# Sigmoid attention followed by a SiLU layer: halves of queries in the first two batches, loads cast by the DMA, q at both row halves, and another order of the second product

## Chip, cores and metric

The kernel runs on one core of one Trainium2 chip. The metric is the device time of one execution in microseconds (us). Times are medians; traces are of one profiled execution, whose span is some 2 us shorter than its time.

## The reference

Eight batches of 12 heads, 448 positions, head width 64; then a layer with 768 inputs, 2048 hidden units, 768 outputs, over 3584 tokens.

```python
scores = scale * np.matmul(q, k.transpose(0, 1, 3, 2)) - np.log(S)
attn = 1.0 / (1.0 + np.exp(-scores))
attn_out = np.matmul(attn, v)                       # (8, 12, 448, 64), inputs float32
x = attn_out.transpose(0, 2, 1, 3).reshape(B * S, H * D)
h = x @ w_in                                        # 3584 x 768 x 2048
out = (h * (1.0 / (1.0 + np.exp(-h)))) @ w_out      # 3584 x 2048 x 768
```

## The kernel before

The kernel works in float16 with float32 sums. Four heads make a group n, three groups a batch, 24 groups in all. For each group TensorE makes seven steps of scores S (four 64 x 64 products side by side in the array), ScalarE the sigmoids of each step (128 x 896), TensorE V (28 matmuls), VectorE moves the result out as xt. G1 is the product of a batch with w_in: 96 matmuls of 448 columns. G2 is the product with w_out for two blocks of 128 tokens; it is done by Strassen's scheme in Winograd's form, with 7 products of 8 matmuls (384 columns), so it needs sums of its inputs (`gs`, VectorE) and combinations of its products (`ua`, `ub`, `uc`, VectorE). There are 14 such pairs. wi and wo are the copies of w_in and w_out that TensorE reads; xk and xq are the loaded k and q, kT and qT their transposes, and k3 means k of group 3.

Where k and q come from: SP loads float32 into a stage, VectorE or GpSimd casts, then the chunks are transposed, by TensorE for groups 0 to 2 and by the DMA afterwards.

```python
def load_qk(b, g):                       # SP queue, float32 stage
    ... nc.sync.dma_start(t, src[b, 4 * g : 4 * g + 4].rearrange(...))
def cast(b, g, eng_name, eng): ...       # 128 x 896, float32 to float16
def transpose_dma(b, g):                 # one per group for q, one for k
    ... nc.sync.dma_start_transpose(tT[nm][n % NT_], x16[nm][n % 1]...)
```

The order of G2's products and of the stages:

```python
prod(1, X, a11, b11, True, ...);  copy X -> ra
prod(6, Y, s2, t2, True, ...);    comb(rb, Y, ra, "u2")
prod(5, Z, s1, t1, True, ...)
prod(2, X, a12, b21, False, ...); copy X -> o1
prod(7, Y, s3, t3, False, [u2]);  comb(rc, Y, ra, "u3"); comb(o2, Z, rc, "c22")
prod(4, Y, a22, t4, False, [u3]); comb(o2, Y, ra, "c21")    # waits for u3 at once
prod(3, Z, s4, b22, False, [c22]); comb(o1, Z, rb, "c12")
...
plan = [("1", 0), ("1", 1), ("2", 0), ("2", 1), ("2", 2), ("1", 2), ("2", 3), ("2", 4), ("1", 3), ("2", 5), ...]
```

TensorE works in order: an instruction that waits holds all behind it. So the order in which the program lists S, V, G1 and G2 decides what a wait costs.

## Time and profile before

| | before |
|---|---|
| time | 436.48 us (436.12 to 436.83) |
| TensorE busy | 385.4 us of 434.4 |
| ScalarE, VectorE busy | 224.1 and 195.0 us |
| batch 0's attention alone | 0 to 40 us |
| end of G1 of batch 1 | 109.6 us |
| last matmul ends | 429.1 us |

How to read the profile: the page cuts the span into 40 slices and gives each engine's busy share in tenths; sums by stage give the busy time between two moments; the waits list says for whom an engine waited (total, times, longest); the timeline lists instructions with the idle time before them in brackets. In the DMA view q0, `software_dynamic`, is GpSimd's queue, and q1, `hardware_dynamic`, is SP's, which has the DMA transposes. The lines themselves stand in the prediction.

### The profile page before, as it was taken

The numbers are of one execution on the slowest core, as the hardware profiler recorded it, in microseconds if no ns is written. First come the engines' busy times: TensorE is split into PE (matmuls) and PEld (weight loads), VectorE is DVE, ScalarE is ACT, GpSimd is POOL, SyncE is SP. The second block draws the span as 40 slices with busy tenths as digits, with TensorE's granted clock in tenths as the row PEclk, the third lists the DMA queues.
The fourth block names the chain that finished last, engine by engine and source line by source line (L and its number), as shares of the span: only waits on it lengthen the run. The fifth ranks groups of instructions, "written<-read, shape, count | busy, mean of one in ns | idle before, by whom it ended". The sixth has DMA issues, their size and how long they took to land.

```text
span 434.4 us, 7192 instructions
## 1 busy us (share of the span) xinstructions
PE 385.4 (89%) x2938; PEld 187.2 (43%) x2938; DVE 195.0 (45%) x298; ACT 224.1 (52%) x326; POOL 69.9 (16%) x92
## 2 busy tenths in 40 slices
PE   2768977799997999899999999989999999899894
PEld 1333533244443444444454444544444454455452
DVE  2321861244553444734455534634563445545642
ACT  1655475587652668456645556457755434014300
POOL 6344013322003213300121022200210000000000
PEclk9856985699998999999999999999999999999999
DMA  8999987797257898718881388717820220031022
GB/s 226 271 238 205 190 155 165 168 152 151 42 156 151 223 191 180 149 21 201 158 212 23 77 163 191 146 17 132 216 44 10 65 74 0 9 92 48 0 73 73
DMA packets 68513, 54.93 MB, mean 126 GB/s; under 512 B 41344, under 2 KB 64896, under 8 KB 68480
## 3 DMA queue, kind: packets, MB, share of 16 engines
q1 hardware_dynamic: 56512, 42.68, 40.5%
q0 software_dynamic: 11968, 11.80, 18.9%
q8 instruction: 23, 0.38, 0.4%
q14 instruction: 10, 0.08, 0.0%
HBM read 45.61 MB, written 11.01 MB: 130 GB/s over the span
## 4 chain that ended last, share of the span: by engine, by line
PE 78%; DVE 9%; ACT 5%; DMA 4%; issue 1%; SPq 1%; POOL 0%; DVEq 0%; POOLq 0%
PE gm L516 34%; PE gm L653 27%; PE att L406 9%; PE att L388 7%; ACT at L398 5%; DVE gs L250 3%; DVE xt L418 3%; DMA stq<-in_q_dram 2%; DVE uc L664 2%; DMA stk<-in_k_dram 2%; DMA kT<-xk 1%; PE gm L315 1%; DVE ob L664 1%; ACT sg L496 0%; SPq L204 0%
## 5 line engine op out<-in xcount | busy, mean ns | idle before, releaser
L398 ACT ACTIVATE at<-att 128x896 f16<-128x896 f32 x168 | 145.0, 917 | 92.1 <-PE att L388 92.1
L516 PE MATMUL gm<-xt,wi 128*128 128x448 f16 x768 | 151.8, 355 | 0.0
L502 DVE TENSOR_TENSOR gt<-gm,sg 128x448 f16<-128x448 f32 x128 | 79.7, 624 | 79.2 <-ACT sg L496 78.9
L496 ACT ACTIVATE sg<-gm 128x448 f16<-128x448 f32 x128 | 70.0, 547 | 74.4 <-PE gm L516 67.1
L516 PEld LDWEIGHTS <-wi 128*128 128x128 f16 x768 | 73.4, 98 | 76.4 <-issue 12.0
L388 PE MATMUL att<-qT,kT 64*64 64x448 f16 x672 | 57.8, 394 | 18.5 <-ACT at L398 9.8
L653 PEld LDWEIGHTS <-gt 128*128 128x128 f16 x448 | 41.3, 98 | 47.8 <-issue 24.0
L653 PE MATMUL gm<-wo,gt 128*128 128x384 f16 x336 | 61.2, 327 | 0.0
L418 DVE TENSOR_SCALAR xt<-att 128x896 f16<-128x896 f32 x24 | 26.2, 1092 | 69.8 <-PE att L406 69.7
L292 POOL CAST xq<-stq 128x896 f16<-128x896 f32 x21 | 19.6, 932 | 215.1 <-DMA stq<-in_q_dram 202.3
L653 PE MATMUL gm<-so,gs 128*128 128x384 f16 x224 | 40.6, 327 | 7.7 <-DVE gs L250 7.5
L653 PEld LDWEIGHTS <-gs 128*128 128x128 f16 x336 | 31.0, 98 | 35.9 <-DVE gs L250 12.3
L406 PE MATMUL att<-at,v 64*64 64x448 f16 x672 | 43.5, 403 | 1.6 <-ACT at L398 1.6
L388 PEld LDWEIGHTS <-kT 64*64 64x64 f16 x672 | 16.5, 110 | 51.6 <-issue 43.5
L406 PEld LDWEIGHTS <-v 64*64 64x64 f16 x672 | 21.7, 119 | 20.6 <-issue 10.2
L653 PE MATMUL gm<-so,gt 128*128 128x384 f16 x112 | 22.8, 338 | 8.5 <-DVE uc L664 8.4
L664 DVE SCALAR_TENSOR_TENSOR uc<-gm,ua 128x384 f32<-128x384 f32 x14 | 7.8, 556 | 40.4 <-PE gm L653 40.4
L292 POOL CAST xk<-stk 128x896 f16<-128x896 f32 x21 | 20.1, 956 | 13.3 <-DMA stk<-in_k_dram 6.8
L653 PE MATMUL gm<-wo,gs 128*128 128x384 f16 x112 | 21.4, 333 | 0.0
L214 POOL DMA_DIRECT2D v<-in_v_dram x24 | 17.5, 729 | 2.4 <-DMA wi<-in_moe_w_in_dram 2.3
L683 ACT ACTIVATE ob<-gm 128x384 f32<-128x384 f32 x14 | 6.9, 495 | 17.6 <-PE gm L653 17.6
L675 ACT ACTIVATE ua<-gm 128x384 f32<-128x384 f32 x14 | 6.9, 492 | 16.1 <-PE gm L653 16.1
(29 smaller groups left out, 112.3 us busy)
## 6 DMA issues: line engine op xcount, KB each, us to landing
stq<-in_q_dram SPq DMA_DIRECT2D x24, 448.0 KB, 5.3
stk<-in_k_dram SPq DMA_DIRECT2D x24, 448.0 KB, 6.0
out_dram<-ob SPq DMA_DIRECT2D x56, 192.0 KB, 2.9
v<-in_v_dram POOLq DMA_DIRECT2D x24, 224.0 KB, 4.7
wi<-in_moe_w_in_dram POOLq DMA_DIRECT2D x16, 192.0 KB, 11.7
wo<-in_moe_w_out_dram POOLq DMA_DIRECT2D x4, 768.0 KB, 16.5
qT<-xq SPq DMA_TRANSPOSE x21, 3.0
kT<-xk SPq DMA_TRANSPOSE x21, 5.2
```

What stands on the lines that cost most here:

```text
L214: lambda: nc.gpsimd.dma_start(v16[b % NV][:, 2 * g : 2 * g + 2], v[b, 4 * g : 4 * g + 4].rearrange("(j h) (p c) d -> (h p) j (c d)", h=2, ...
L250: return lambda: eng.tensor_tensor(o, a, b_, op)
L292: lambda xi=xi, t=t, e_=e_: e_.tensor_copy(xi.rearrange("p c j d -> p j c d"), t.rearrange("p j (c d) -> p j c d", c=NCH)),
L388: nc.tensor.matmul(pt[64 * h : 64 * h + 64, j, :S], kT[64 * j : 64 * j + 64, s, 64 * h : 64 * h + 64], qT[64 * j : 64 * j + 64, :, 64 * h ...
L398: lambda: nc.scalar.activation(av[:, :, s, :], pt[:, :, :S], AF.Sigmoid, bias=NEG_LOG_S, scale=QKSCALE),
L406: nc.tensor.matmul(pt[64 * j : 64 * j + 64, h, :S], v16[b % NV][64 * h : 64 * h + 64, 2 * g + j, c * D : (c + 1) * D], av[64 * h : 64 * h ...
L418: lambda: nc.vector.tensor_scalar_mul(x[:, 2 * g : 2 * g + 2, :], pt[:, :, :S], SX),
L496: lambda: nc.scalar.activation(t, src, AF.Sigmoid, scale=ISX),
L502: lambda: nc.vector.tensor_tensor(o, src.rearrange("p (a t) -> p a t", t=cn), t.rearrange("p (a t) -> p a t", t=cn), ALU.mult),
L516: nc.tensor.matmul(bank[:, :S], wi[:, cc, fc * P : (fc + 1) * P], x[:, cc, :], start=(cc == 0), stop=(cc == NCC - 1),)
L653: nc.tensor.matmul(bank[:, :HE], lhs[:, c, :], rhs[:, c, :], start=first and c == 0, stop=(c == HFC - 1), skip_group_check=True,)
L664: lambda: nc.vector.scalar_tensor_tensor(o, bank[:, :HE], ISX, u, ALU.mult, ALU.add), prio=-1,
```

## The change

Five things are changed together:

1. In batches 0 and 1 the queries are done in two parts, 256 and 192, so that G1 of the first part can start while the second part's attention is still going on.
2. q and k are loaded by GpSimd's queue with a cast by the DMA; the stage and 48 casts vanish, and loads run several groups ahead.
3. Without the cast the chunks can't be rearranged, so each chunk of q must lie at both row halves of the array. For that q is transposed twice, the second time shifted by 64 columns: three DMA transposes per group (7 + 7 + 8 chunks) in place of two.
4. In G2 product 7 stands ahead of product 2; the sums for a pair are queued ahead and are made inside the pair before; no pair directly follows the G1 that it reads.
5. Warm-up matmuls on zeros, 7 at the start and 19 where waits are expected.

The core of the diff (condensed: helpers, buffer counts and the planning code are cut):

```diff
-                pl.op("SP", 60, ("st", nm, b, g), ...,
-                    lambda t=t, src=src: nc.sync.dma_start(t, src[b, 4 * g : 4 * g + 4].rearrange(...)))
+    def load_k(n): ... nc.gpsimd.dma_start(xk[n % NX]..., src(k, b, g))
+    def load_q(n, part=None): ... nc.gpsimd.dma_start(xq[n % NX][:, D : D + 2 * S]..., src(q, b, g)[:, :, lo:hi])
...
+    def transpose_dma(n):
+        nc.sync.dma_start_transpose(kT[n % NTR], xk[n % NX])
+        nc.sync.dma_start_transpose(qT[n % NTR][:, 1 : NCK : 2], xq[n % NX][:, D : D + 2 * S])
+        nc.sync.dma_start_transpose(qT[n % NTR][:, 0 : NCK + 1 : 2], xq[n % NX])
...
-        prod(2, X, a12, b21, False, [kk("a")])
         prod(7, Y, s3, t3, False, ...)
+        prod(2, X, a12, b21, False, [kk("a")])
         prod(4, Y, a22, t4, False, [kk("u3")] ...)
...
+    order_in = [('k', 0), ('id',), ('q', 0, 0), ('k', 1), ..., ('wi', 0), ('wi', 1), ('wi', 2),
+                ('n', 3), ('n', 4), ('n', 5), ('wo', 0, 4), ('wo', 8, 12), ...]
+    todo += [('S', 0, 0, 0), ..., ('V', 2, 1), ('S', 3, 0, 0), ..., ('S', 4, 0, 0), ('V', 3, 0), ...]
+    items += [G2(0), G2(1), G1(2), G2(2), G2(3), G1(3), G2(4), G2(5), G1(4), G2(6), ...]
```

`order_in` is the order on the GpSimd queue; ('n', 3) loads k, q, v of group 3 and queues its three transposes on SP. `todo` is the attention of batches 0 and 1 in steps, laid between the blocks of G1.

## The prediction

> **What bounds the kernel now.** I read the page's 40 slices first, then the sums by stage, the chain of waits, the waits of TensorE after 110 us, and the DMA packets. The program is: 24 groups n (8 batches of 3, four heads each) of attention, S (scores) then V; a first product G1 per batch (96 matmuls of 448 columns); then G2, 14 pairs of output blocks at 56 matmuls of 384 columns.
>
> ```profile
> PE   2768977799997999899999999989999999899894
> ACT  1655475587652668456645556457755434014300
> PEclk9856985699998999999999999999999999999999
> DMA  8999987797257898718881388717820220031022
> ```
>
> Slices are 10.9 us. TensorE is full from the eleventh on, at nearly full clock. The loss lies in the first ten slices and in small gaps later. The sums by stage (busy us of TensorE, weight loads, VectorE, ScalarE, GpSimd; then the clock, DMA share, GB/s):
>
> ```profile
> 0.00:40.00 40.00, 22.91 (x211) 11.21 (x212) 9.41 (x14) 19.28 (x23) 19.55 (x33) 0.77 1.10 238
> 40.00:59.00 19.00, 19.00 (x96) 9.45 (x95) 14.83 (x21) 8.16 (x15) 2.07 (x3) 0.95 1.12 170
> 59.00:85.00 26.00, 18.09 (x170) 7.46 (x170) 5.59 (x7) 18.06 (x22) 6.46 (x9) 0.63 0.80 178
> 85.00:110.00 25.00, 25.00 (x184) 10.95 (x183) 12.39 (x19) 18.97 (x30) 6.64 (x8) 0.98 0.82 147
> 110.00:430.00 320.00, 300.40 (x2282) 148.14 (x2280) 152.75 (x239) 159.59 (x238) 35.20 (x41) 0.99 0.47 104
> ```
>
> Up to 40 us there is batch 0's attention alone, then G1 of batch 0 alone, from 59 to 85 us batch 1's attention alone; only from 85 us on do attention and products lie side by side. In both lonely attention stages ScalarE works 18 to 19 us, and TensorE is half used and cold. The chain of waits shows the hand-offs in the first:
>
> ```profile
> 13.83 3.35 ACT at L398 x4
> 17.23 2.28 PE att L406 x28
> 19.60 1.10 DVE xt L418
> 20.75 0.59 PE att L388 x4
> ```
>
> Later TensorE idles 19.6 us of the 320 between 110 and 430, mostly here (total, times, longest):
>
> ```profile
> PE gm L653 <- DVE uc L664: 8.4, 12, 1.0
> PE gm L653 <- DVE gs L250: 7.5, 7, 1.5
> PE att L388 <- DMA kT<-xk: 2.4, 1, 2.4
> ```
>
> So there are about 45 us to win at the start and 18 later. After the last matmul some 4.4 us of store remain in any case.
>
> **What the Trainium skill says.** TensorE: Matmul & The Clock Gate, Part 1, gives half clock until about 3.4 us of sustained work, and again after an idle window. The trace agrees: the clock row falls to 0.5 to 0.6 in the attention stages. The same page, Back-to-back issue gap, gives N/2.4 + 2.5 ns for an isolated stream, 189 ns at 448 columns: 12 matmuls of G1 take 2.38 us in the chain (198 ns each with one change to attention and back), so I take its form for 256 and 192 columns as an estimate, 109 and 83 ns. DMA: Bandwidth & Descriptors, section SWDGE vs HWDGE vs iDMA, says that a cast needs the GpSimd path, a DMA transpose the other, and that each DMA engine goes round-robin between the queues. The trace agrees to the packet. Between 41 and 54 us wo streams on the GpSimd queue while two transposes wait on the other:
>
> ```profile
> q0 software_dynamic: 1425, 2.13, 94.4%
> q1 hardware_dynamic: 1418, 0.35, 23.1%
> ```
>
> One transpose packet goes through per wo packet. A transpose has 896 packets of 256 bytes; alone, 928 packets were done in about 1.4 us (68.0 to 69.4 us), here 109 per us, 8 us a transpose. This decides my number.
>
> **The change, part by part.**
>
> 1. *Halves of queries in batches 0 and 1.* Part 0 has 256 queries, part 1 has 192. The order of instructions puts part 0 of groups 0 to 2 first, then G1 of batch 0 part 0 with part 1's attention between its blocks, then G1 part 1 with groups 3 to 5 part 0, then G1 of batch 1 part 0 with their part 1, then G1 of batch 1 part 1 with group 6. First S: k0 and q0 are now issued behind the identity at about 1.4 us and land near 5 and 6; two sets of transposes and two copies put S at about 8.5, against 10.5 before. Part 0 is 3584 sigmoid elements per partition per group; 1792 elements cost 1.66 us by two of the old 0.83 us instructions, and instructions are fewer, so 3.7 us a group plus 0.4 for V's hand-off: 12.3 us for three, end at 21, G1 starts near 23 (before: 40). G1 part 0: 96 x 109 ns = 10.5 us, S and V of part 1 in it 4.4, some 15 changes at 0.24 us 3.6: 18 us. The weights wi land for good at about 31 (27 us of loads at the 200 to 213 packets per us seen when the GpSimd queue is alone), costing 1 to 2 us: end about 42. Next stage likewise about 18, then 18, then G1 part 1 (8.0) with group 6 and changes, 12.5. If every load were there: 42 + 18 + 18 + 12.5 = 90 us. In the kernel before the end of G1 of batch 1 is at 109.5, with six steps of S more done (1.8 us).
>
> 2. *Warm-up matmuls* (7 at the start and some in later waits) keep the clock up; they stand in idle time and cost nothing by themselves.
>
> 3. *Casts by the DMA.* 48 casts leave GpSimd and VectorE (0.93 us each on GpSimd, off the path except for 0.95 in the chain). q and k now go on the GpSimd queue, 256 packets each, at 0.73 us of issue per DMA; 82 DMAs are 60 us of GpSimd time, hidden. The loads run up to four groups ahead, so the one stall at 130 us (2.4) goes.
>
> 4. *q at both row halves* turns two DMA transposes per group into three (7 + 7 + 8 chunks, 2816 packets); 63 in place of 42. Alone that is 4.2 us per group against about 13 us of TensorE work per group: hidden later. Not at the start. Group 3's transposes can begin when k3 lands, about 33 us. Behind it the GpSimd queue has k4 to v5 and all of wo, about 1600 packets at 125 per us in turns (estimated from the v loads, which got 119 to 129) and 2048 at 109 to 113. Taken strictly in turns group 3 is ready at 33 + 13 + 11 = 57 us (wanted at 42); group 4, with the loads of groups 6 and 7 in its way, near 79; group 5 near 90. From group 5 on 37.5 us of work follow to the end of G1 of batch 1 (5 for its part 0, 20 for the next stage, 12.5): 127 us. That would lose 18 us instead of winning 20.
>
> 5. *G2's order and early sums.* The order is now products 1, 6, 5, 7, 2, 4, 3, so a product lies between each combination and the one that needs it (1.3 us, against 0.57 + 0.04 of VectorE); the sums of the next pair start inside the last, and in the plan no pair directly follows the G1 that it reads. So 8.4 + 7.5 + 2.4 = 18.3 us go. From 109.5 on: 324.9 - 18.3 + 1.8 = 308.4, plus 2 for new small waits: 310.
>
> Sum: 90 + 310 = 400 with free transposes, 127 + 310 = 437 with strict turns. I choose group 5 ready at 68 us, between: GpSimd issues at most eight loads ahead and pauses, in which transposes run at full speed, and a kernel with so finely ordered loads was probably fitted on a chip. Then 68 + 37.5 = 105.5, and 105.5 + 310 = 415.
>
> **The rivals.**
> - *The transposes take the place of the wait removed* (437, strict turns). For it: the two equal packet counts, and 50% more transposes. Against it: in the kernel before, groups 3 and 4 still came through by 63.7 us beside wo.
> - *Loads hidden, ScalarE and TensorE balanced* (about 400). For it: slack of the later DMA, whose share after 110 us is 0.47. Against it: DMA share above 1 for the whole first 59 us.
> - *Small matmuls bound by weight loads.* A weight load is 98 ns in the table, a 192-column matmul 83: 96 x 2 x 15 ns = 3 us more. Against it: with 448 columns loads overlap freely. It would add 3 to any of the above.
> - *G2 waits come back* through the one set of sums or the eight result buffers: up to 8 us.
>
> **Range and chances.** I give 40% to about 400 (395 to 410), 35% to the middle (410 to 426), 25% to strict turns (426 to 440). Faster by 2% means under 427.7. Range 394 to 436; faster 0.73, within 2% 0.23, slower 0.04.
>
> **What would show it right or wrong.** Right: G1 starts near 23 us; TensorE waits for DMA transposes qT or kT at groups 3, 4 and 5, between 40 and 70 us, with equal packet counts of both queues; G1 of batch 1 ends at about 105; waits of G2 for uc and gs fall from 15.9 to under 3 us; TensorE idles under 5 us after that. Wrong, to the good: no transpose wait over 2 us, time about 400. Wrong, to the bad: group 5's scores start past 85 us, or the G2 waits stay.

## More of the kernel before

One trap matters later: a matmul's end is modelled. A matmul of 384 columns is recorded with 326 ns although the next one starts 163 ns after it.

## The result

| | before | after |
|---|---|---|
| time, median of 4 | 436.65 us | 425.56 us (424.53 to 425.98) |
| span of the profiled run | 434.4 us | 423.7 us |
| G1 of batch 0 starts | 39.9 us | 22.5 us |
| end of G1 of batch 1 | 109.6 us | 121.9 us |
| from there to the end | 324.8 us | 301.8 us |

The ratio is 0.9744, with a 95% interval of 0.9724 to 0.9764. A ratio is the mean time of one kernel's runs over that of the other's of the same rounds, so it is not quite the ratio of the medians quoted.

The changed kernel starts G1 17 us earlier, yet it ends G1 of batch 1 12 us later; then it wins 23 us. The page of the changed kernel shows where, with the same four rows as before (a slice is now 10.6 us):

```profile
PE   7998013799999999999999999999999999999995
ACT  2865003477775567546655577667645656034100
PEclk9999658699999999999999999999999999999999
DMA  8999999949999983869746998651322100330143
```

TensorE is nearly full in the first four slices, which is the gain that was meant. In slices 5 and 6 (counted from 0) all engines nearly stand still, while the DMA row stays at 9; slices 7 and 8 have a second, smaller hole. From slice 9 on TensorE is at 9 until the last slice. The sums by stage, in the same columns as before:

```profile
0.00:22.50 22.50, 19.80 (x300) 11.10 (x300) 7.61 (x21) 12.55 (x15) 17.46 (x31) 1.00 1.09 159
22.50:41.00 18.50, 17.51 (x260) 11.32 (x256) 7.02 (x11) 11.26 (x18) 9.07 (x14) 1.00 1.22 196
41.00:61.50 20.50, 0.01 (x1) 0.01 (x1) 2.08 (x3) 0.60 (x1) 2.65 (x4) 0.59 1.18 199
61.50:122.00 60.50, 50.60 (x693) 34.88 (x694) 25.95 (x40) 36.23 (x56) 12.86 (x18) 0.89 1.13 148
122.00:419.00 297.00, 296.79 (x2308) 148.84 (x2306) 149.48 (x237) 162.92 (x243) 22.93 (x32) 1.00 0.54 97
```

Between 41 and 61.5 us TensorE does 0.01 us of work. After 122 us it idles 0.2 us of 297. The longest of what TensorE waited for, by the waits list of the whole span (the four left out are 0.4 us and less):

```profile
PE att L407 <- DMA qT<-xq: 29.9, 2, 20.5
PE gm L841 <- DVE warm L195: 1.2, 1, 1.2
PE gm L346 <- DMA xk<-in_k_dram: 0.7, 1, 0.7
PE gm L579 <- DMA wi<-in_moe_w_in_dram: 0.7, 1, 0.7
```

The waits of G2 for `uc` and `gs` are gone from the list. In their place stand two waits for the transposed q, groups 3 and 4. The timeline of SP's queue gives each DMA transpose's issue (start, duration); three lines are a group, k then q then q shifted:

```profile
33.18 1.33 SPq L325 DMA_TRANSPOSE kT<-xk  x1
34.57 4.57 SPq L329 DMA_TRANSPOSE qT<-xq  x1
39.19 9.37 SPq L333 DMA_TRANSPOSE qT<-xq  x1
48.68 7.66 SPq L325 DMA_TRANSPOSE kT<-xk  x1
...
77.10 1.24 SPq L325 DMA_TRANSPOSE kT<-xk  x1
78.45 1.43 SPq L329 DMA_TRANSPOSE qT<-xq  x1
```

Group 3's first transpose is issued as soon as k3 has landed (33.1 us), and its last has landed at 61.4 us. Over the whole run the median of an issue is 1.25 to 1.31 us; here it takes up to 9.4. I read this as the issue itself standing in line behind packets that move slowly; no run tests that. The DMA view between 41 and 54 us, the same window as the prediction showed of before (queue: packets, MB, share):

```profile
q0 software_dynamic: 1605, 2.19, 94.3%
q1 hardware_dynamic: 1605, 0.39, 24.1%
```

The two counts are equal. Counted over 36 to 60 us the transposes got 2818 packets, about the 2816 of one group, the first at 37.1 us. Between 76 and 78 us, when GpSimd's queue moves only 25 packets, the transposes get 2091 in 2 us.

The kernel before had transposes as slow as this: those of group 3 landed at 50.4 and 57.7 us. But there G1 of batch 0 kept TensorE busy until 59.1 us, so nobody waited. The change asks for the same group at 41 us.

### The profile page after: what moved, and what is told of

It is laid out like the page before. It is cut to its first block, busy times and chain, and to the rows that moved or that the text cites. A ratio compares the mean times of both kernels' runs of the same rounds, so it can differ in the third digit from the quotient of the medians. Undisturbed runs are those within 1.5% of the kernel's fastest.

```text
span 423.7 us, 8550 instructions
## 1 busy us (share of the span) xinstructions
PE 384.7 (91%) x3555; PEld 206.1 (49%) x3555; DVE 192.5 (45%) x311; ACT 223.5 (53%) x332; POOL 65.0 (15%) x97
## 4 chain that ended last, share of the span: by engine, by line
PE 82%; DMA 10%; SPq 4%; POOL 1%; DVE 1%; issue 1%; ACT 1%; POOLq 0%; ACTq 0%
PE gm L579 34%; PE gm L665 31%; PE att L407 9%; PE att L419 8%; DMA wi<-in_moe_w_in_dram 4%; DMA qT<-xq 4%; SPq L325 2%; DMA v<-in_v_dram 2%; SPq L333 1%; SPq L329 1%; POOL xk L215 1%; POOL xq L224 0%; DVE gs L272 0%; ACT at L812 0%; ACT sg L537 0%
## 5 line engine op out<-in xcount | busy, mean ns | idle before, releaser
L579 PE MATMUL gm<-xt,wi 128*128 128x448 f16 (+2 forms) x960 | 161.8, 319 | 1.0 <-DMA wi<-in_moe_w_in_dram 0.7
L451 ACT ACTIVATE at<-att 128x896 f16<-128x896 f32 x126 | 109.6, 916 | 55.1 <-PE att L407 54.9
L542 DVE TENSOR_TENSOR gt<-gm,sg 128x448 f16<-128x448 f32 (+2 forms) x128 | 79.7, 624 | 128.0 <-ACT sg L537 128.0
L537 ACT ACTIVATE sg<-gm 128x448 f16<-128x448 f32 (+2 forms) x128 | 69.7, 547 | 45.0 <-PE gm L579 41.6
L407 PE MATMUL att<-qT,kT 64*64 64x448 f16 (+2 forms) x840 | 55.9, 332 | 30.5 <-DMA qT<-xq 29.9
L812 ACT ACTIVATE at<-att 128x1024 f16<-128x1024 f32 (+3 forms) x48 | 38.5, 824 | 51.3 <-PE att L407 50.9
L679 DVE SCALAR_TENSOR_TENSOR us<-gm,us 128x384 f32<-128x384 f32 x70 | 38.8, 554 | 43.7 <-PE gm L665 36.9
L419 PE MATMUL att<-at,v 64*64 64x448 f16 (+2 forms) x840 | 38.4, 320 | 0.3
L224 POOL DMA_DIRECT2D xq<-in_q_dram x27 | 19.6, 726 | 35.3 <-DMA qT<-xq 27.8
L215 POOL DMA_DIRECT2D xk<-in_k_dram x24 | 17.4, 726 | 11.2 <-DMA kT<-xk 5.3
```

Of the source, the lines that this page charges most:

```text
L215: lambda: nc.gpsimd.dma_start(xk[n % NX].rearrange("p (j c) -> p j c", j=2), src(k, b, g)),
L224: lambda: nc.gpsimd.dma_start(xq[n % NX][:, D : D + 2 * S].rearrange("p (j c) -> p j c", j=2)[:, :, lo:hi], src(q, b, g)[:, :, lo:hi],),
L407: nc.tensor.matmul(pt[64 * h : 64 * h + 64, r, lo : lo + (c1 - c0) * D], kT[n % NTR][64 * r : 64 * r + 64, i, 64 * h : 64 * h + 64], qT[n ...
L419: nc.tensor.matmul(pt[64 * j : 64 * j + 64, h, :N], v16[n % NV][64 * h : 64 * h + 64, j, c * D : (c + 1) * D], at[64 * h : 64 * h + 64, sl ...
L451: lambda: nc.scalar.activation(at[:, sl], pt[:, :, :S], AF.Sigmoid, bias=NEG_LOG_S, scale=QKSCALE),
L537: lambda: nc.scalar.activation(t[:, :ncol], src_, AF.Sigmoid, scale=ISX), prio=0,
```

## The experiments

Twelve kernels ran, four together each time, each with three rounds. All were correct. The three calls ran on different chips, so across calls compare the ratios. A planner in the program lays out the queues by estimated times, so an edit may also shift an order that it doesn't name; that was not checked. Medians of the kernel before: 435.58 (e1 to e4), 434.32 (e6 to e9), 434.83 us (e5, e10 to e12).

| label | what | median us | ratio to before, 95% interval |
|---|---|---|---|
| (changed) | the change itself | 425.56 | 0.9744, 0.9724 to 0.9764 |
| e1_pe6 | changed, groups 3 to 5 transposed by TensorE | 400.50 | 0.9215, 0.9153 to 0.9277 |
| e2_wo_late | changed, wo behind groups 6 to 8 | 419.48 | 0.9665, 0.9595 to 0.9734 |
| e3_before_order | before, edit in unused code | 435.09 | 1.0008, 0.9956 to 1.0060 |
| e4_before_g2 | before, order of stages only | 432.61 | 0.9945, 0.9888 to 1.0002 |
| e5_nhb1 | changed, batch 1 whole | 421.34 | 0.9705, 0.9656 to 0.9754 |
| e6_before_order | before, product order only | 429.58 | 0.9889, 0.9848 to 0.9929 |
| e7_before_g2 | before, all of the new G2 | 418.64 | 0.9648, 0.9592 to 0.9704 |
| e8_after_oldorder | changed, old product order | 435.23 | 1.0002, 0.9959 to 1.0046 |
| e9_nowarm | changed, no warm-ups | 424.70 | 0.9774, 0.9736 to 0.9812 |
| e10_pe6_nowarm | e1 without warm-ups | 400.49 | 0.9228, 0.9198 to 0.9258 |
| e11_pe6_nhb1 | e1 with batch 1 whole | 405.98 | 0.9339, 0.9316 to 0.9363 |
| e12_pe5 | e1, group 5 back to the DMA | 411.26 | 0.9459, 0.9444 to 0.9474 |

### What holds TensorE between 41 and 77 us: e1, e2, e12

**e1_pe6.** Groups 3 to 5 are transposed on TensorE, as 0 to 2 are.

```diff
-    NPE = 3
+    NPE = 6
-    ... ('S', 3, 0, 0), ('S', 3, 0, 2), ('S', 3, 0, 4), ('S', 3, 0, 6), ... ('S', 4, 0, 4), ('S', 4, 0, 6), ...
+    ... ('t', 3), ('S', 3, 0, 0), ('S', 3, 0, 2), ('S', 3, 0, 4), ('t', 4), ('S', 3, 0, 6), ... ('S', 4, 0, 4), ('t', 5), ('S', 4, 0, 6), ...
```

> The changed kernel with groups 3, 4 and 5 transposed by TensorE (as groups 0 to 2 are) in place of the DMA. Theory (transposes starve because they share each DMA engine packet by packet with the loads and wo): the waits of 20.5 and 9.4 us at groups 3 and 4 vanish, some 5 us of transposes are added on TensorE, G1 of batch 1 ends near 95 us in place of 121.8, time 397 to 402 us. Rival (the loads of groups 3 to 5 themselves land too late, so that the transposes are not at fault): waits of 15 us or more stay at group 3, now for xk or xq, time 420 or more.

Measured: 400.50 us, within the expected 397 to 402. G1 of batch 1 ends at 95.4 us; the mean clock is 0.999. The largest wait of TensorE left for a DMA is

```profile
PE att L407 <- DMA qT<-xq: 1.2, 1, 1.2
```

and that is group 6. So the transposes held TensorE. That the loads were in time shows in the changed kernel's own trace too: k3 and q3 landed at 33.1 and 34.3 us, and the last load of groups 3 to 5 at 45.9, long before TensorE got them transposed (61.4, 76.6 and 79.5 us). Three groups of transposes cost TensorE 0.55 + 0.97 us each, 4.6 us, and took away waits of 29.9.

**e2_wo_late.** The same loads in another order, so that wo comes after loads which have to wait for free buffers.

```diff
-('n', 5), ('wo', 0, 4), ...
+('n', 5), ('n', 6), ('n', 7), ('n', 8), ('wo', 0, 4), ...
-    for n in range(2 * NQ, NALL):
+    for n in range(9, NALL):
```

> The changed kernel with the loads of groups 6 to 8 ahead of wo, so that wo, held behind loads that reuse buffers, streams only after group 4's transposes. Theory (turns are taken with whatever stands on the GpSimd queue): group 3 is ready near 53 us (61.5 before), group 4 near 66 (76.6), G1 of batch 1 ends near 112, time 414 to 418 us. Rival (the transposes are slow by themselves, whatever else moves): group 3 and group 4 as before, time within 2 us of 425.6, or later if wo then comes late for G2.

Measured: 419.48 us, a little outside the expected 414 to 418. The timeline of TensorE shows both waits:

```profile
54.28 0.64 PE L407 MATMUL att<-qT,kT 64*64 64x256 f16 x8 [12.99 <-DMA qT<-xq]
...
76.96 0.64 PE L407 MATMUL att<-qT,kT 64*64 64x256 f16 x8 [10.75 <-DMA qT<-xq]
```

Group 3 came at 54.3 us (61.5 in the changed kernel), as expected. Group 4's last transpose landed at 56.6, earlier than I had expected. The second wait is for group 5: by then wo had been let go (it was issued at 58.6 us), and group 5's last transpose, issued at 57.5, landed at 76.9. So the delay follows wo, to where wo is put: group 4 comes 20 us earlier with wo out of its way. That speaks against transposes that are slow by themselves. What I missed was that wo would meet group 5.

**e12_pe5.** As e1, but group 5 stays with the DMA (`NPE = 5`, without `('t', 5)`).

> The fast variant with group 5 given back to the DMA transposes (3 and 4 stay on TensorE). Theory (turn by turn with wo): its 2816 packets begin at about 41 us and need some 20 us beside v5 and wo at 112 to 125 per us, so group 5 is ready at 61 to 63 us, wanted at 56: a wait of 5 to 7 us, against 2 us of transposes saved: 402 to 406 us. Rival (two groups fewer in the queue make it ready in time): 397 to 399 us.

Measured: 411.26 us; one wait, of 14.4 us, up to 68.2 us where I expected 5 to 7 up to 61 to 63. The DMA view from 45 to 65 us:

```profile
q0 software_dynamic: 2415, 3.05, 93.2%
q1 hardware_dynamic: 2411, 0.60, 27.8%
```

Turn by turn again. My count of the other queue was short: with groups 3 and 4 transposed on TensorE their buffers come free early, so the loads of groups 6 and 7 follow wo without a pause, and the transposes take turns with these too. 2816 packets at 112 to 125 per us are 23 to 25 us, which from about 44 us on gives 67 to 69. One group left to the DMA cost 10.8 us, against 1.5 us on TensorE.

### What G2's order is worth: e3, e4, e6, e7, e8

**e3_before_order** was meant to move product 7 ahead of product 2 in the kernel before.

> The kernel before with one thing changed: G2's product 7 ahead of product 2. Theory (a product between a combination and its reader hides it): the wait for uc, 8.4 us, falls to under 1; the wait for gs, 7.5, stays; time 427 to 429 us. Rival (the wait moves to the next product of the bank): under 3 us gained.

Measured: 435.09 us, nothing, and waits for `uc` of 8.4 us as ever. The edit had fallen into a function with nearly the same text that this kernel never calls, so the run compares the kernel before with itself: ratio 1.0008. It tells nothing of the order and is a check of the method.

**e4_before_g2** had, for the same reason, only the other order of stages (`plan`).

```diff
-    plan = [("1", 0), ("1", 1), ("2", 0), ("2", 1), ("2", 2), ("1", 2), ("2", 3), ("2", 4), ...]
+    plan = [("1", 0), ("1", 1), ("2", 0), ("2", 1), ("1", 2), ("2", 2), ("2", 3), ("1", 3), ...]
```

> The kernel before with the product order of the changed kernel and its order of stages (no G2 pair directly behind the G1 that it reads). Theory: both waits go, 8.4 + 7.5 us, time 419 to 422 us, which is below the changed kernel's 425.6. Rival (the sums then collide with the evictions of G1 on VectorE, or attention is paced worse): 425 or more.

Measured: 432.61 us. The waits for `gs` fall from 7.5 to 4.3 us, those for `uc` stay at 7.6. The order of stages alone is not clear of noise.

**e6_before_order** is e3's edit in the right function.

```diff
-        prod(2, X, a12, b21, False, [kk("a")])
         prod(7, Y, s3, t3, False, [kk("u2")] + sk[:3])
+        prod(2, X, a12, b21, False, [kk("a")])
```

> The kernel before with product 7 ahead of product 2 in the G2 that really runs (the edit of e3 had fallen into an unused function, so that e3 was the kernel before once more). Theory (a product between a combination and its reader hides it): the wait for uc, 8.4 us in 12 pieces, goes to under 1, the wait for gs (7.5) stays, time 425 to 429 us. Rival (e3's reading at face value: the order is worth nothing): within 2 us of the kernel before.

Measured: 429.58 us, just above the expected range, ratio 0.9889. The kernel's waits after 110 us:

```profile
PE att L388 <- DMA kT<-xk: 7.1, 6, 2.1
PE gm L653 <- DVE gs L250: 6.9, 7, 1.4
```

The wait for `uc` is gone. Part of the gain was given back: attention in this kernel, which loads one group ahead, now waits longer for its transposes (7.1 us where it was 2.4). I take the quicker G2 as the cause.

**e7_before_g2** adds the order of stages and sums queued ahead for all pairs.

```diff
+    for pi in range(NG // 2):
+        g2_fast(pi, 0.0, True)          # queues the sums only
```

> The kernel before with all of the changed kernel's treatment of G2: product order, order of stages, and sums queued ahead so that VectorE makes them inside the previous pair. Theory: start-to-start times of G2's matmuls fall from a mean of 192 to 163 ns, 19.7 us in all, time 415 to 419 us, below the changed kernel, since the start is left as it was. Rival (the waits move to evictions and VectorE): 425 or more.

Measured: 418.64 us, ratio 0.9648. From start to start, matmuls within G2 take 163 ns in the mean, where the kernel before takes 192: 120.4 us over 738 intervals against 140.7 over 733. The same two products, first in the kernel before, then in the changed kernel, where the spacing is as in e7:

```profile
422.91 2.76 PE L653 MATMUL gm<-wo,gt 128*128 128x384 f16 x16
426.32 1.46 PE L653 MATMUL gm<-so,gt 128*128 128x384 f16 x8 [0.65 <-DVE uc L664]
...
404.32 2.76 PE L665 MATMUL gm<-wo,gt 128*128 128x384 f16 x16
406.92 1.46 PE L665 MATMUL gm<-so,gt 128*128 128x384 f16 x8
```

From start to start that is 3.41 us against 2.60: a wait listed with 0.65 us cost 0.81. In the waits list after 110 us a single line is left, the DMA again:

```profile
PE att L388 <- DMA kT<-xk: 5.1, 3, 2.7
```

So with the old start and the new G2 the kernel before beats the changed kernel (the intervals of the two ratios don't overlap).

**e8_after_oldorder** takes only the product order back in the changed kernel.

```diff
+            self.prod(2, X, a12, b21, False, [kk("a")])
             self.prod(7, Y, s3, t3, False, [kk("u2")] + sk[3])
-            self.prod(2, X, a12, b21, False, [kk("a")])
```

> The changed kernel with product 2 ahead of product 7 again, all else kept. Theory: about 0.8 us per pair for 14 pairs come back as waits for us (the combination), time 434 to 437 us. Rival (it is the early sums alone that took the waits away): under 428 us.

Measured: 435.23 us, ratio 1.0002. The waits for the combinations are back (7.5 us in 11 pieces), the mean from start to start in G2 is 175 ns. Taking back the moved product alone costs about what the whole change gained.

### Warm-ups and halves: e9, e10, e5, e11

**e9_nowarm** drops all 26 warm-up matmuls from the changed kernel.

> The changed kernel without its 26 warm-up matmuls. Theory (up to group 3 the time is set by the DMA, not by TensorE): group 3 still starts at 61 to 62 us though TensorE is cold before, time within 2 us of 425.6. Rival (the clock at the start counts): 2 to 6 us longer.

Measured: 424.70 us. G1 starts at 23.5 instead of 22.5 us, and group 3 at 61.1: so a start that is 1 us later has no bearing on the time, since the DMA sets when group 3 comes. The warm-ups do bring the full clock earlier: seven transposes took 0.56 us at 14.6 us with them, 0.93 at 15.2 us without.

**e10_pe6_nowarm** drops them from e1.

> The fast variant (groups 3 to 5 transposed by TensorE) without warm-up matmuls. Theory: once no transposes by DMA stand in the way the start is set by TensorE and ScalarE, so a cold clock shows: 1 to 5 us longer than that variant, 401 to 406 us, with a clock under 1.0 before 25 us. Rival (the wait for the weights wi at 32 us hides it): within 1 us.

Measured: 400.49 us; here the rival was right. G1 starts at 23.6 instead of 22.3 us but ends at 95.5 instead of 95.4. The wait of 1.0 us for wi that e1 has at 32 us is no longer listed: TensorE comes later to weights that land when they land. In the same way e1's wait of 1.2 us for group 6 has gone from the list. The expected clock under 1.0 doesn't show as such: the windows view gives 1.00 up to 40 us, but seven transposes still take 0.93 us at 15.1 us.

**e5_nhb1** leaves batch 1 whole (`NHB = 1`, groups 3 to 5 removed from `todo`), so that G1 of batch 0 no longer stands behind group 3.

> The changed kernel with batch 0 alone in halves, batch 1 whole. Theory (the DMA sets when groups 3 to 5 are ready: 61, 77 and 80 us, whatever TensorE does): G1 of batch 0 part 1 (8 us) now runs inside the wait for group 3, group 3's scores still begin at 60 to 62 us, the wait shrinks to about 11 us, and the halves of batch 1 prove to have been of no use: 418 to 424 us. Rival (batch 1's halves are worth what batch 0's are): 430 or more.

Measured: 421.34 us, as expected in the total. One step was wrong: the wait for group 3 did not shrink. It is 20.8 us and again ends at 61.5, because all of part 1 of G1 stands behind group 3's first score here too. It is the later waits that shrank: 3.0 us at 77 us and 0.5 at 94, as group 3's attention with G1's part 1 between its scores (61.5 to 74.0 us) fills the time to group 4's transposes, and group 4's attention that to group 5's. So while transposes are late, no gain from the halves of batch 1 can be seen.

**e11_pe6_nhb1** does the same to e1.

> The fast variant with batch 1 whole. Theory: the halves of batch 1 pay once the DMA is out of the way, since otherwise batch 1's attention stands alone again, some 19 us of ScalarE with TensorE half idle: 6 to 12 us longer than the fast variant, 405 to 412 us. Rival: the halves cost as much in small matmuls as they hide, within 2 us.

Measured: 405.98 us, 5.5 us over e1, at the lower edge of what I expected. With transposes out of the way the halves of batch 1 pay.

## Why the prediction was right or wrong

The range held (394 to 436), and the direction was right. The time of 425.6 lies 10.6 us over the 415 given. Of that, the start was too hopeful by 16.4 us (121.9 for 105.5) and the rest too cautious by 8.2 (301.8 for 310). The other 2.4 us are no error in the kernel's parts: the sum adds up stages of the trace, and so gives a span, which is 1.8 us shorter than the time, and 415.5 was rounded to 415. That two errors in part cancelled is luck. The case given the best chance (40% to about 400) did not come.

1. **Up to the first wait: right.** G1 was to start near 23 us (22.5), its first part to end at about 42 (41.0), with 1 to 2 us of waiting for wi (0.7). Casts, loads ahead and halves together did what was argued; they were not measured one by one.
2. **The start without late transposes: right.** It was to end at 90 us. e1 ends at 95.4 with 4.6 us of transposes added, so by subtraction at 90.8 without.
3. **Transposes in turns: right in kind, and the step "I choose group 5 ready at 68 us, between" failed.** Strict turns gave 57, 79 and 90 us for groups 3, 4, 5. They came at 61.4, 76.6 and 79.5. Group 3 came 4 us after the strict count; its first packet moved only 3.9 us after the issue (1.2 us in quiet stretches). Groups 4 and 5 came earlier, as GpSimd's queue paused: it held q7 until 62 us and q8 until 77 us, each waiting for the transposes that read its buffer. I had both pieces of evidence before me, the equal packet counts and the count of packets ahead of each group, and moved away from them because so finely ordered a kernel "was probably fitted on a chip". That reason had no measurement behind it. The sum was also hung on the wrong group: the wait for group 4 is the last one for a DMA, and from it 45.2 us follow (76.7 to 121.9). So G1 of batch 1 ended at 121.9, not 105.5: 11.5 us because group 5 came at 79.5 and not 68, and 4.9 because 42.4 us followed from there and not 37.5.
4. **G2: right in kind, too small in size.** 18.3 us were to go and 2 to come. From the end of G1 of batch 1 on 301.8 us were measured, where 310 were given. The term that was off is the sum of listed waits: 8.4 + 7.5 us. A wait is listed from the modelled end of the last matmul, which lies some 160 ns after the moment at which the next could have started. From start to start the kernel before has 21 long gaps in G2, which take 19.2 us more than the usual 163 ns each. It has also ten matmuls about 320 ns apart after the wait of 2.4 us at 134 us (the clock was 0.87 between 130 and 140 us), 1.5 us more. The changed kernel and e7 have neither. The 2 us for new small waits did not come: TensorE idles 0.2 us.
5. **Casts and warm-ups: right.** The wait at 130 us is gone. The warm-ups bring the clock up earlier and cost nothing, and by e9 and e10 they gain no time.
6. **Rivals.** Transposes in the place of the wait removed: this is what happened, half hidden by the better G2. Small matmuls bound by weight loads: no. In e1 the median from start to start is 109 ns at 256 columns and 83 ns at 192, as estimated, beside weight loads of 98 ns. G2 waits come back: no, none is listed.
7. **Sums and readings.** The "about 45 us to win at the start" have no working: the table shows 25 us of idle TensorE before 110 us. The 82 DMAs on GpSimd are 91 in the trace. The store after the last matmul is 5.3 us (434.4 - 429.1), not 4.4. A group's part 0 is put at 3.7 us, although four instructions of 0.83 us make 3.3. "To the packet" was 1425 against 1418. None of these moves the 415: the number for a group, 4.1 us with its hand-off, came near the 4.3 us measured between groups.

Put together from the runs: the new G2 is worth 3.5% (e7 against before). The new start is worth nothing as built, for e7, with the old start, is at 0.9648 against 0.9744 of the change; and it is worth much once groups 3 to 5 do not use the DMA transpose (e1, 0.9215). Open remains why group 3's first transpose packet needs 3.9 us after its issue, and how the casts, the halves and the double q divide the gain at the start, since they depend on each other and were not separated.

## What to carry to other kernels

Count the packets that stand in the other queue when a transfer becomes urgent: here a transpose of many small packets shared with large loads packet by packet, and took as long as they did. While the DMA is full, try the transposes on TensorE (29.9 us of waits for 4.6 of work here), or keep bulk loads that nobody needs yet out of that time. And put an independent product between a combination and the product that reads it, then measure what it is worth from start to start of the matmuls.

## What the Trainium skill lacked or had wrong

- DMA: Bandwidth & Descriptors, section SWDGE vs HWDGE vs iDMA, says that an engine goes round-robin between queues, and this holds: 1605 packets against 1605 in 13 us. No page gives the size of the consequence for a DMA transpose: a packet of 256 bytes waits a turn for one of 896 or 1536, so about 2816 of them took 23 us, where 2091 took 2 us with the other queue nearly still.
- The same page, section Issuing engines are not separate DMA queues, calls the issue time "usually small relative to the DMA itself". Here the issue of one DMA transpose on SP grew from 1.3 to 9.4 us while GpSimd's queue was full, of 22.2 us from issue to landing. "Usually" leaves room for this; the page lacks the case.
- TensorE: Matmul & The Clock Gate, section Back-to-back issue gap, gives N/2.4 + 2.5 ns for an isolated matmul and about 131 ns at 512 columns in streams with weight loads. These streams have a weight load for each matmul and keep to the first form: medians of 189, 163, 109 and 83 ns at 448, 384, 256 and 192 columns. The 131 ns do not fit: 384 columns already take 163. A stream of 512 columns with weight loads was not run.
- Perfetto Trace Analysis, section Identifying the Most-Contended Engine, warns that matmul busy time is a bad measure. It lacks by how much waits are understated: recorded 326 ns, spacing 163 ns at 384 columns; 15.9 us of listed waits in G2 stood for 19.2.
